# A limit of three on the loads under way in an agent-attention and soft-MoE kernel

## The chip, the cores and the metric

The kernel runs on one core of a Trainium2 chip. The core has engines that run side by side, each with its own instruction stream: TensorE for matrix products (PE in the profile; PEld is its loading of weights), VectorE (DVE), ScalarE (ACT), GpSimd (POOL) and SyncE (SP). Here SP computes nothing: it issues all DMAs, which move data between the device's memory and the on-chip memory on 16 DMA engines. The metric is the device time of one execution in microseconds (us); a lower one is better.

## The reference

Four batches (B = 4) of 11,456 rows with 128 channels pass through an agent attention with 49 agents, and all 45,824 rows of its result through a soft mixture of eight experts. Everything is in float32. Cut to what matters:

```python
def _attn_ref(q, k, v, agents):
    def sm(a, b):                       # softmax of scaled scores over the last axis
        s = scale * (a @ b.transpose(0, 2, 1))
        e = np.exp(s - s.max(-1, keepdims=True))
        return e / (e.sum(-1, keepdims=True) + 1e-09)
    a2k = sm(agents, k)
    agent_v = a2k @ v
    q2a = sm(q, agents)
    return q2a @ agent_v

def _moe_ref(x, phi, w1, w2):
    logits = x @ phi                    # N x 32 slots
    d = softmax of logits over the N rows
    slot_input = (d.T @ x).reshape(8, 4, 128)
    for e in range(8):
        slot_out[e] = np.maximum(slot_input[e] @ w1[e], 0.0) @ w2[e]
    c = softmax of logits over the 32 slots
    return c @ slot_out
```

## The kernel before, in words

A batch is cut into 90 cells of 128 rows. The k and v of a batch are read in five groups of up to 20 cells (`KGROUPS`), q in six groups of up to 16 (`GROUPS`). A group of k or of q is loaded transposed, 128 channels by cells x 128 rows, 64 KB a cell; a group of v has 129 columns a row, 64.5 KB a cell. There are 20 groups each of k and v, and 24 of q.

For each k group TensorE computes scores against the agents (`ks`, line 252), VectorE a running maximum, ScalarE the exponentials, and TensorE multiplies these with v (`kE`, line 351). For each q group TensorE computes scores (`qs`, line 466), the softmax over the agents follows on VectorE, ScalarE and GpSimd, then transposes (line 522) and the logits of the mixture (line 535). Rounds of two q groups or one gather the slots' inputs. When the last batch is through, the experts run (`mh`, line 805, with w1; `mo`, line 834, with w2), and a last loop forms the output and stores it in pieces of up to 1 MB (lines 994 to 1008).

The order of all steps is written out by hand in `ORDER`. Each token there is a step of one engine, and each engine takes its own steps in that order. `kx`, `kv` and `qx` are the loads of a k, v and q group, `cx` a load of constants, `w1` and `w2` those of the experts' weights. All go through SP, in order.

A load of a group is issued as DMAs of at most seven cells: 7, 7 and 6 cells for k and v (448, 448 and 384 KB, for v 451.5, 451.5 and 387), 7, 7 and 2 for q (448, 448 and 128 KB); a group of ten cells is 7 and 3. The function `load` (line 238) does it for k and q, `kv_` (line 285) for v:

```python
        for c0 in range(0, n, 7):
            c1 = min(c0 + 7, n)
            nc.sync.dma_start(out=xt[:, P * c0:P * c1],
                              in_=src[b, :, P * (ca + c0):P * (ca + c1)])
```

The buffers are few: two for k groups, three for v and three for q (`BUFS`: kt, vt, qt). A load into a buffer waits on SP until the last reader of what was there before is through; that reader is TensorE. Each DMA tells of its landing on one of eight semaphores, taken in turn, and before SP issues a DMA it waits for the one that used the semaphore before. The weights of the experts come at the end of the load stage: w1 and w2 each in four DMAs of 1 MB, two experts apiece, three of those of w2 into q buffers.

Of the kernel before, what the change touches and what calls it, by code (L numbers as in the profile page):

```python
# [17 lines left out]
P = 128  # L18
# [109 lines left out]
    "s": 4, "a": 3, "m": 1, "hs": 2, "ht": 3,  # L128
}
DEN_ACT = tuple(range(0, B * NG, 2))  # L130
FILL = (0, 4, 4, 3, 4, 3, 2)
CHUNKS = [4, 12] + [16] * 21 + [4, 4]
C0 = [sum(CHUNKS[:j]) for j in range(len(CHUNKS))]
# [40 lines left out]
def tile_agent_attn_soft_moe(ctx, tc, qT, kT, vL, agT, phi, w1, w2, cst, out):  # L174
    nc = tc.nc
# [48 lines left out]
    def op(fam, i, eng, cost, fn, deps=(), takes=(), gives=()):  # L224

        k = (fam,) + tuple(i)
        ops[k] = {"eng": eng, "cost": cost, "deps": list(dict.fromkeys(deps)), "takes": takes,
                  "gives": gives, "reads": {}}
        for tag, first in gives:
            ops[first]["reads"][tag] = ops[first]["reads"].get(tag, 0) + 1  # L230
        fns[k] = fn
        return k

    def tile_(tag, shape, name):
        return pools.get(tag, rp).tile(shape, F32, name=name,
                                       tag=f"{tag}{slots[tag, now[0]].pop(0)}", bufs=1)

    def load(tag, src, b, ca, cb, most):
        xt = tile_(tag, [P, most * P], f"{tag}_{b}_{ca}")
        n = cb - ca  # L240
        for c0 in range(0, n, 7):
            c1 = min(c0 + 7, n)
            nc.sync.dma_start(out=xt[:, P * c0:P * c1],
                              in_=src[b, :, P * (ca + c0):P * (ca + c1)])
        return xt

    def scores(b, xt, c0, c1, nm):

        sp = tile_("s", [P, c1 - c0, A], f"s{nm}")
        for c in range(c0, c1):  # L250
            for r in range(0, P, 64):
                t_.matmul(sp[r:r + 64, c - c0, :], xt[:, P * c + r:P * c + r + 64], ag[:, b, 0:A],  # L252
                          start=True, stop=True)
        return sp
# [12 lines left out]
    def k_ops(i):  # L267
        b, g = kgroups[i]
        ca, cb = KGROUPS[b][g]
        n, last = cb - ca, cb == NCELL  # L270
        cut = [(0, min(10, n))] + ([(10, n)] if n > 10 else [])
        k = {}
# [3 lines left out]
        def kx():  # L276
            if i:
                k["x"] = load("kt", kT, b, ca, cb, KC)
                return
            k["x"] = tile_("kt", [P, KC * P], "kt_0")  # L280
            for c0, c1 in ((ca, 4), (4, cb)):
                nc.sync.dma_start(out=k["x"][:, P * c0:P * c1], in_=kT[b, :, P * c0:P * c1])
            nc.sync.dma_start(out=cs[:, :P], in_=cst[:, :P])

        def kv_():
            k["v"] = tile_("vt", [P, KC, VC], f"vt_{i}")
            for c0 in range(0, n, 7):
                c1 = min(c0 + 7, n)
                nc.sync.dma_start(out=k["v"][:, c0:c1, :], in_=vL[b, :, ca + c0:ca + c1, :])

        def ks_(h):
            k["s", h] = scores(b, k["x"], *cut[h], f"k_{i}_{h}")
# [99 lines left out]
        def o(fam, sub, eng, cost, fn, **kw):  # L392
            return op(fam, (i,) + sub, eng, cost, fn, **kw)

        x = o("kx", (), "D", 156 * n, kx, takes=("kt",))
        v = o("kv", (), "D", 157 * n, kv_, takes=("vt",), deps=(x,))
        hs_ = range(len(cut))
        nh = [c1 - c0 for c0, c1 in cut]
# [43 lines left out]
    def q_ops(i):  # L442
# [17 lines left out]
        def qx():  # L460
            q["x"] = load("qt", qT, b, ca, cb, QC)[:, :P * n].rearrange("p (r x) -> p r x", r=4)
# [13 lines left out]
        def qm():  # L475
            q["mx"] = sm.tile([P, QC], F32, name=f"mx_{i}", tag="mx", bufs=6)
            v_.tensor_reduce(out=q["mx"][:, :n], in_=q["pt"][:, :n, 0:A], axis=AX.X, op=ALU.max,  # L477
                             negate=i in DEN_ACT)

# [103 lines left out]
        es, ps_, cc = [], [], []  # L583
        if i in DEN_ACT:
            for h in range(2):
# [101 lines left out]
    z, hps, hts, sos, w2s = {}, {}, {}, {}, {}  # L687
# [10 lines left out]
    def wl(name, shape, **kw):  # L698
        return z["wp"].tile(shape, F32, name=name, **kw)

    def z_w1(x):
        if x == 0:
            z["w1"] = wl("w1s", [P, E, F])
        nc.sync.dma_start(out=z["w1"][:, 2 * x:2 * x + 2, :], in_=w1[x])

    def z_w2(x):
        w2s[x] = (tile_("qt", [P, 2, F // P, C], f"w2s{x}") if x < 3 else
                  wl(f"w2s{x}", [P, 2, F // P, C]))
        nc.sync.dma_start(out=w2s[x], in_=w2[x])

    def z_ms():
        z["so"] = wl("so", [P, 2, C])
# [155 lines left out]
    def z_fl(n):  # L868
        fl = tile_("s", [P, 2, P], f"fl_{n}")
        for x in range(2):  # L870
            t_.transpose(fl[:, x], ident, ident)
# [9 lines left out]
    for x in range(4):  # L881
        wx.append(o("w1", "D", 2500, lambda x=x: z_w1(x), deps=ends + wx[-1:]))
    for x in range(4):
        wy.append(o("w2", "D", 2500, lambda x=x: z_w2(x), takes=("qt",) if x < 3 else (),
                    deps=ends + [("qx", NT - 1)] + wy[-1:]))
# [75 lines left out]
    f = None  # L961
    for n, d in enumerate([("qs", NT - 1, 1)] * FILL[0] + [("ql", NT - 1)] * FILL[1] +
                          [("r2", NR - 1)] * FILL[2] + [("r3", NR - 1)] * FILL[3] +
                          [w_] * FILL[4] + [gl] * FILL[5] + [b1] * FILL[6]):
        f = op("fl", (n,), "P", 214, lambda n=n: z_fl(n), deps=(d, f) if f else (d,),
# [103 lines left out]
```

## Time and profile before

| | |
|---|---|
| Median of three runs | 319.85 us (319.0 to 320.51) |
| The profiled execution | 321.17 us, its span 318.9 us |
| Busy PE, DVE, ACT, POOL in the span | 84%, 78%, 59%, 42% |
| Read from and written to the device's memory | 79.91 MB and 23.59 MB |
| Mean granted clock of TensorE | 0.931 |

The span is the time from the first to the last instruction of the profiled execution. It has three stages: to about 205 us loads and attention, to about 258 us the last rounds and the experts, and then the output. A row of the view by stretch gives, after the stretch's start and end, its length, the busy time of each engine with the number of its instructions, the granted clock, the share of the 16 DMA engines' time that was used (a little over 1 is full), and GB/s. A row of waits names who waited, for whom, the sum in us, how often and the longest. A row of DMA issues gives what is written from what, the number, the size of one and the median time from issue to landing. A row of the timeline gives the start, the length and the instruction. In the view of a line or a tile a row gives least, median and largest duration of an instruction in ns, and the first and the last start in us.

### The profile page before, as it was taken

The numbers are of one execution on the slowest core, as the hardware profiler recorded it, in microseconds if no ns is written. First come the engines' busy times: TensorE is split into PE (matmuls) and PEld (weight loads), VectorE is DVE, ScalarE is ACT, GpSimd is POOL, SyncE is SP. The second block draws the span as 40 slices with busy tenths as digits, with TensorE's granted clock in tenths as the row PEclk, the third lists the DMA queues.
The fourth block names the chain that finished last, engine by engine and source line by source line (L and its number), as shares of the span: only waits on it lengthen the run. The fifth ranks groups of instructions, "written<-read, shape, count | busy, mean of one in ns | idle before, by whom it ended". The sixth has DMA issues, their size and how long they took to land.

```text
span 318.9 us, 11055 instructions
## 1 busy us (share of the span) xinstructions
PE 266.3 (84%) x4522; PEld 169.4 (53%) x4522; DVE 248.1 (78%) x598; ACT 189.4 (59%) x623; POOL 132.5 (42%) x166
## 2 busy tenths in 40 slices
PE   3799999997698998988999998998898876766850
PEld 3638668665554776664666775565574632111210
DVE  1357767897769986988999988988999659989830
ACT  1125791492754985558589568698663255655550
POOL 1012223064505552566444490476897404434300
PEclk9999999999989999999999999999999997767555
DMA  7999999999979999867996899746930049999997
GB/s 250 400 402 390 398 396 402 401 397 400 394 250 376 399 393 368 301 260 295 377 377 264 252 360 384 244 175 237 419 141 3 2 164 422 415 415 420 420 419 286
DMA packets 31298, 104.20 MB, mean 327 GB/s; under 512 B 3601, under 2 KB 7825, under 8 KB 27537
## 3 DMA queue, kind: packets, MB, share of 16 engines
q1 hardware_dynamic: 31248, 103.52, 84.4%
q8 instruction: 35, 0.57, 0.7%
q14 instruction: 15, 0.11, 0.1%
HBM read 79.91 MB, written 23.59 MB: 325 GB/s over the span
## 4 chain that ended last, share of the span: by engine, by line
PE 45%; DVE 26%; DMA 10%; ACT 9%; issue 5%; POOL 2%; SPq 0%; DVEq 0%; POOLq 0%; ACTq 0%
PE sk L252 10%; PE ev L351 8%; PE sq L466 8%; DMA out<-ot 7%; PE tp L522 5%; ACT pt L494 4%; PE po L1002 3%; DVE pt L472 3%; PE lq L535 3%; DVE kmx L305 2%; ACT ot L1007 2%; DVE cd L852 2%; DVE ot L1006 2%; DMA w1s<-w 2%; DVE mx L477 2%
## 5 line engine op out<-in xcount | busy, mean ns | idle before, releaser
L494 ACT ACTIVATE pt<-pt,mx 128x49 f32<-128x49 f32 x192 | 61.6, 329 | 10.2 <-DVE mx L477 10.2
L513 POOL TENSOR_TENSOR pt<-pt,rt 128x392 f32<-128x392 f32 (+1 forms) x48 | 38.7, 809 | 46.1 <-DVE rt L508 25.2
L252 PE MATMUL sk<-ag,kt 128*64 128x49 f32 x1440 | 51.7, 230 | 6.6 <-DMA kt<-kT 4.3
L252 PEld LDWEIGHTS sk<-ag,kt 128*64 128x64 f32 x1440 | 48.8, 145 | 11.6 <-DVE ag L183 4.1
L466 PE MATMUL sq<-qt,ag 128*32 128x512 f32 (+1 forms) x384 | 49.6, 607 | 1.8 <-DVE et L339 1.1
L1002 PE MATMUL po<-ct,sob 32*128 32x512 f32 (+2 forms) x200 | 37.8, 838 | 15.6 <-DVE ct L865 11.3
L351 PE MATMUL ev<-vt,et 128*64 128x129 f32 x720 | 46.8, 277 | 1.7 <-issue 1.4
L1007 ACT COPY ot<-po 128x1536 f32<-128x1536 f32 (+2 forms) x25 | 32.8, 1311 | 23.3 <-DVE ot L1006 23.2
L351 PEld LDWEIGHTS ev<-vt,et 128*64 128x64 f32 x720 | 40.3, 138 | 9.6 <-issue 5.6
L472 DVE STREAM_TRANSPOSE pt<-sq 128x512 f32<-128x512 f32 (+1 forms) x48 | 31.9, 669 | 12.5 <-PE sq L466 12.0
L635 POOL TENSOR_TENSOR dt<-x_all,mbs 128x512 f32<-128x512 f32 (+1 forms) x24 | 29.2, 1227 | 28.8 <-DVE mbs L626 24.9
L859 POOL TENSOR_TENSOR x_all<-x_all,cd 128x512 f32<-128x512 f32 (+2 forms) x25 | 24.0, 961 | 38.0 <-DVE cd L854 37.3
L482 POOL TENSOR_TENSOR pt<-pt,mx 128x784 f32<-128x784 f32 (+1 forms) x12 | 16.2, 1353 | 55.4 <-DVE mx L477 53.1
L494 ACT ACTIVATION_READ_ACCUMULATOR pt<-pt,mx 128x1 f32 x192 | 37.0, 193 | 0.0
L529 ACT COPY pT<-tp 128x512 f32<-128x512 f32 (+1 forms) x48 | 25.7, 557 | 13.1 <-PE tp L522 11.0
L1002 PEld LDWEIGHTS po<-ct,sob 32*128 32x128 f32 x200 | 10.8, 247 | 42.5 <-ACT ot L1007 42.1
L522 PE MATMUL tp<-cs,pt 128*128 128x128 f32 x180 | 27.9, 286 | 5.9 <-issue 4.2
L305 DVE TENSOR_REDUCE kmx<-sk 128x49 f32<-128x490 f32 x32 | 20.7, 658 | 13.8 <-PE sk L252 13.6
L344 ACT ACTIVATE et<-et 128x490 f32<-128x490 f32 x36 | 21.6, 619 | 11.2 <-DVE et L339 11.1
L522 PEld LDWEIGHTS tp<-cs,pt 128*128 128x128 f32 x180 | 19.5, 142 | 15.1 <-issue 9.0
L339 DVE TENSOR_TENSOR et<-sk,kmb 128x490 f32<-128x490 f32 x36 | 22.5, 653 | 2.9 <-ACT kmb L329 2.8
L1006 DVE COPY ot<-po 128x512 f32<-128x512 f32 (+2 forms) x25 | 15.7, 629 | 11.4 <-DMA out<-ot 7.5
(111 smaller groups left out, 396.6 us busy)
## 6 DMA issues: line engine op xcount, KB each, us to landing
out<-ot SPq DMA_DIRECT2D x21, 1024.0 KB, 7.4
qt<-qT SPq DMA_DIRECT2D x44, 448.0 KB, 7.4
vt<-vL SPq DMA_DIRECT2D x36, 451.5 KB, 7.4
kt<-kT SPq DMA_DIRECT2D x35, 448.0 KB, 6.7
kt<-kT SPq DMA_DIRECT2D x17, 384.0 KB, 6.9
vt<-vL SPq DMA_DIRECT2D x16, 387.0 KB, 8.1
w2s<-w SPq DMA_DIRECT2D x4, 1024.0 KB, 6.9
w1s<-w SPq DMA_DIRECT2D x4, 1024.0 KB, 10.5
```

The costliest lines, as they stand in the source:

```text
L252: t_.matmul(sp[r:r + 64, c - c0, :], xt[:, P * c + r:P * c + r + 64], ag[:, b, 0:A], start=True, stop=True)
L305: v_.tensor_reduce(out=o_, in_=sp.rearrange("p c a -> p a c"), axis=AX.X, op=ALU.max)
L351: t_.matmul(k["ev"][o_:o_ + 64, :], k["e"][:, c, :], k["v"][:, c, :], start=c < 2, stop=c >= n - 2)
L466: t_.matmul(q["s", h][32 * r_:32 * r_ + 32, :nt], ag[:, b, 32 * h:32 * h + 32], q["x"][:, r_, :], start=True, stop=True)
L472: v_.transpose(out=q["pt"][:, :n, 32 * h:32 * h + 32], in_=q["s", h][:, :nt].rearrange("p (t a) -> p t a", a=32))
L494: s_.activation(out=x, in_=x, func=AF.Exp, bias=q["mx"][:, c:c + 1], accum_out=q["dn"][:, c:c + 1])
L513: nc.gpsimd.tensor_tensor(out=x, in0=x, op=ALU.mult, in1=q["rt"][:, c0:c1].unsqueeze(2).to_broadcast([P, c1 - c0, A]))
L522: t_.transpose(q["tp", h][:, (c - c0) // 2, :], q["pt"][:, c:c + 2, :].rearrange("p c a -> p (c a)"), ident)
L529: s_.copy(out=q["pT"][:, c0 // 2:c1 // 2, :], in_=q["tp", h][:, :(c1 - c0) // 2, :])
L635: nc.gpsimd.tensor_tensor(out=q["dt"][:, :n], in0=q["lt"][:, :n, :], op=ALU.subtract, in1=mbs[:, ri, :].unsqueeze(1).to_broadcast([P, n, S]))
L1002: t_.matmul(po[:, r, :32 * n], z["sob"][32 * r:32 * r + 32, :], z["ct", j][32 * r:32 * r + 32, :32 * n], start=True, stop=True)
L1007: s_.copy(out=ov[:, 1:4], in_=po[:, 1:4, :32 * n])
```

## The change

A list of the loads sent is kept. Every DMA of k, q, v, w1 and w2 goes through a new function `send`, which makes it wait until the one three places ahead of it in that list has landed. The DMAs of the agents and the constants and the stores do not go through it. The DMAs of w1 and w2 are cut in two, one for each expert, 512 KB each. Sizes and order of the other loads, buffers and `ORDER` stay.

```diff
+AHEAD = 3
@@
+    sent = []
+
+    def send(out, in_):
+
+        i = nc.sync.dma_start(out=out, in_=in_)
+        i = getattr(i, "ins", i)
+        if len(sent) >= AHEAD:
+            tc.add_manual_dep(i, sent[-AHEAD].name, mybir.DependencyInfo(
+                mybir.DependencyClass.Sync, mybir.DependencyReason.DATA), reason="load queue")
+        sent.append(i)
+
@@ def load
-            nc.sync.dma_start(out=xt[:, P * c0:P * c1],
-                              in_=src[b, :, P * (ca + c0):P * (ca + c1)])
+            send(xt[:, P * c0:P * c1], src[b, :, P * (ca + c0):P * (ca + c1)])
@@ def kx
-                nc.sync.dma_start(out=k["x"][:, P * c0:P * c1], in_=kT[b, :, P * c0:P * c1])
+                send(k["x"][:, P * c0:P * c1], kT[b, :, P * c0:P * c1])
@@ def kv_
-                nc.sync.dma_start(out=k["v"][:, c0:c1, :], in_=vL[b, :, ca + c0:ca + c1, :])
+                send(k["v"][:, c0:c1, :], vL[b, :, ca + c0:ca + c1, :])
@@ def z_w1
-        nc.sync.dma_start(out=z["w1"][:, 2 * x:2 * x + 2, :], in_=w1[x])
+        for e in range(2):
+            send(z["w1"][:, 2 * x + e], w1[x, :, e])
@@ def z_w2
-        nc.sync.dma_start(out=w2s[x], in_=w2[x])
+        for e in range(2):
+            send(w2s[x][:, e], w2[x, :, e])
```

## The prediction

> **What bounds the kernel now.** I first read the head of the page and its chain of waits, then the busy time by stretch.
>
> ```profile
> span 318.9 us, 11055 instructions
> ...
> PE 45%; DVE 26%; DMA 10%; ACT 9%; issue 5%; POOL 2%; SPq 0%; DVEq 0%; POOLq 0%; ACTq 0%
> ```
> ```profile
> core 0: us, PE busy (x) PEld busy (x) DVE busy (x) ACT busy (x) POOL busy (x), PEclk, DMA share, GB/s
> 0.00:30.00 30.00, 22.02 (x312) 15.54 (x312) 12.47 (x24) 6.66 (x21) 4.48 (x13) 1.00 0.96 360
> 30.00:88.00 58.00, 51.42 (x1060) 38.30 (x1062) 44.11 (x104) 36.25 (x148) 19.67 (x25) 0.99 1.03 397
> ...
> 88.00:130.00 42.00, 39.13 (x725) 27.57 (x727) 34.77 (x83) 28.14 (x116) 15.34 (x21) 0.97 0.96 358
> 130.00:157.00 27.00, 24.18 (x507) 15.93 (x507) 23.96 (x60) 17.73 (x61) 15.84 (x17) 1.00 0.82 301
> 157.00:205.00 48.00, 46.12 (x926) 31.21 (x920) 44.22 (x99) 35.86 (x149) 24.30 (x29) 1.00 0.87 313
> ```
>
> The chain is mostly PE, then DVE. By stretch, two things are nearly full at once: PE is busy 51.42 of 58 us and 46.12 of 48 us, and the DMA engines are full from 30 to 88 us (share 1.03, 397 GB/s) and nearly so to 130 us. After that the loads need only 301 to 313 GB/s. So PE sets the pace, with the loads just ahead of it: anything that lowers the rate of the loads below what these stretches ask will be seen.
>
> Next come the waits of SP, which issues all loads, and how many loads are under way at a time.
>
> ```profile
> SPq L243 <- PE sk L252: 21.1, 6, 6.5
> SPq L243 <- DMA kt<-kT: 17.5, 26, 1.4
> ```
> ```profile
> DMA packets 1334, 3.70 MB, mean 403 GB/s; under 512 B 148, under 2 KB 336, under 8 KB 1333
> ...
> vt<-vL SPq DMA_DIRECT2D x4, 451.5 KB, 8.0
> kt<-kT SPq DMA_DIRECT2D x2, 448.0 KB, 8.2
> ```
>
> SP already waits for landings, often and briefly (26 times, 1.4 us at most), and at other times for buffers that PE frees. The second fence is the DMA view of 53.3 to 62.5 us: a load lands 8.0 to 8.2 us after its issue while 403 GB/s flow. 8.1 us of that is 3.26 MB, some seven loads of 448 KB (0.459 MB). The kernel thus has seven or eight loads under way, and the change leaves three.
>
> **The change part by part.** *The wait.* It adds no work to a compute engine. What counts is how long a load takes when little is ahead of it, because with three under way each load is issued when the third before it has landed. The trace has seven such loads, issued after SP had stood waiting for a buffer and the queue had run low. They were issued at 174.77, 130.11, 199.88, 91.07, 144.07, 179.39 and 186.56 us; the first row places the first of them, and the others are in that order, issue to landing in the last column:
>
> ```profile
> 174.77 1.28 SPq L243 DMA_DIRECT2D kt<-kT  x3
> ```
> ```profile
> kt<-kT SPq DMA_DIRECT2D x1, 448.0 KB, 3.5
> ...
> vt<-vL SPq DMA_DIRECT2D x1, 451.5 KB, 3.3
> ...
> qt<-qT SPq DMA_DIRECT2D x1, 448.0 KB, 3.4
> ...
> qt<-qT SPq DMA_DIRECT2D x1, 448.0 KB, 3.3
> ...
> kt<-kT SPq DMA_DIRECT2D x1, 448.0 KB, 4.5
> ...
> vt<-vL SPq DMA_DIRECT2D x1, 451.5 KB, 4.2
> ...
> kt<-kT SPq DMA_DIRECT2D x1, 448.0 KB, 4.2
> ```
>
> Four take 3.3 to 3.5 us and three take 4.2 to 4.5. A 448 KB load takes 0.459 MB / 403 GB/s = 1.14 us of the engines' time, so a quiet load has about 2.2 us in which nothing of its own moves. Two others cover that only if they are large: 448 and 448 KB are 2.28 us, 448 and 384 KB 2.11, but 448 and 128 KB (the tail of a q group) only 1.46.
>
> The rate under the new limit follows. SP issues these loads:
>
> ```profile
> L243 SPq DMA_DIRECT2D qt<-qT x68: 327/328/1147, 5.9 to 200.7; - x68
> L243 SPq DMA_DIRECT2D kt<-kT x54: 327/328/597, 2.6 to 187.4; - x54
> L243 SPq EVENT_SEMAPHORE  x29: 17/17/28, 14.6 to 195.3; - x29
> ...
> L289 SPq DMA_DIRECT2D vt<-vL x56: 327/430/1519, 4.0 to 189.6; - x56
> ```
>
> With the first two of k that is 180 loads. By the kernel's sizes they carry 360 cells of 65,536 bytes for q, the same for k, and 66,048 bytes a cell for v: 70.96 MB, 0.394 MB a load, 1.183 MB for three. A group is read as 448, 448 and 384 or 128 KB, so the first load of a group nearly always waits for the first of the group before, both 448 KB, and three loads cannot land in less than one such time. At 3.4 us that is 1.183 / 3.4 = 348 GB/s; at 3.3 us 358; at 3.5 us 338; at the mean of all seven rows, 3.77 us, 314. I take 348, the middle of the quiet rows.
>
> Now the lag of the loads against before. To 88 us 30 x 360 + 58 x 397 = 33.8 MB were moved, which at 348 GB/s needs 97.2 us: 9.2 us late. From 88 to 130 us 15.0 MB need 43.2 us for 42: 10.4 us late. From 130 to 157 us 8.1 MB need 23.4 for 27, so up to 3.6 us can be won back, if SP's buffers are free. From there 313 GB/s is below 348 and the lag grows no more.
>
> What of it reaches PE is the lag less the time by which loads were early, and that is short in places. Issue, time to landing and first reader of the middle load of two q groups:
>
> ```profile
> 48.23 0.33 SPq L243 DMA_DIRECT2D qt<-qT  x1
> ...
> 148.53 0.44 SPq L243 DMA_DIRECT2D qt<-qT  x1
> ```
> ```profile
> qt<-qT SPq DMA_DIRECT2D x1, 448.0 KB, 7.4
> ...
> qt<-qT SPq DMA_DIRECT2D x1, 448.0 KB, 7.7
> ```
> ```profile
> 56.47 0.64 PE L466 MATMUL sq<-qt,ag 128*32 128x512 f32 x4
> ...
> 156.61 1.08 PE L466 MATMUL sq<-qt,ag 128*32 128x512 f32 x8
> ```
>
> 48.23 + 7.4 = 55.6 against 56.47: 0.9 us early. 148.53 + 7.7 = 156.2 against 156.61: 0.4 us. At 56 us the lag is (10.8 + 26 x 0.397 = 21.1 MB at 348 GB/s) 60.7 - 56 = 4.7 us, so PE would stand 3.8 us; by 157 us it has stood between 6.8 - 0.4 = 6.4 (all won back) and 10.4 - 0.4 = 10 us (nothing). I take 9, near the upper end: PE frees the buffers for which SP waits, and PE is itself late by then. Each third load also passes one more wake-up of SP (17 ns for the semaphore instruction): 60 x 0.02 = 1.2 us. Loads of the 4.2 us kind I charge at two more, about 0.9 us each over the quiet ones: 1.8. Sum: 9 + 1.2 + 1.8 = 12 us. The ends by the same sum: at 358 GB/s the lag at 157 us is 2.2 to 6.5 us, so 2 us at least; at 314 it is 19.7 at 88 us, 25.6 at 130 and about 24.5 at 157 and 205, so 25 us at most.
>
> Behind a waiting load SP holds only the later loads, the constants and, at the end, the stores; no other engine issues a DMA. The constants (two DMAs of lines 676 and 677, 336 and 16 KB by the kernel's sizes) don't pass through the limit and let it rise to five once, worth 0.36 MB / 403 GB/s = 0.9 us at most.
>
> *The halves of w1 and w2.* Eight DMAs of 1 MB become sixteen of 512 KB.
>
> ```profile
> L805 PE MATMUL hp<-w1s,si x32: 592/592/617, 244.7 to 250.1; 128*32 128x512 f32 x32
> L704 SPq DMA_DIRECT2D w1s<-w x4: 328/447/461, 217.3 to 219.9; - x4
> ...
> DMA to landing us min/median/max: 4.7/10.5/16.0
> ```
>
> The last w1 lands at 219.9 + 16.0 = 235.9 us; PE reads it from 244.7: 8.8 us to spare. Six MB go out from 217.3 us; at 348 instead of 403 GB/s these take 2.5 us more. I cost this at nothing: the softmax rounds of batch 3, in PE and DVE, hide it; without them it is 2.5 us. The order of all loads stays, and buffers are neither added nor taken.
>
> The profiled execution took 321.17 us (span 318.9 and 2.3 around it), 1.3 over the median of 319.85. Its sum is 333.2; against the median, which I predict, 319.85 + 12 = 332.
>
> **The rivals.** *Hidden anyway: 320 us.* Part of a load's fixed time may pass while the other two move, since the rows above are loads after a pause. For it: the first load of all, on an idle queue,
>
> ```profile
> ag<-agT SPq DMA_DIRECT2D x1, 128.0 KB, 2.2
> ```
>
> has 2.2 - 0.33 = 1.9 us that isn't its own bytes; 1.9 + 1.14 = 3.0 us gives 390 GB/s, 33.8 MB need 86.7 us and there is no lag. Against it: the four quiet 448 KB rows, none under 3.3. The Trainium skill, "DMA: Bandwidth & Descriptors", section "Anatomy of one DMA — SWDGE (gpsimd) path", fits 2.0 us plus the bytes at 436 GB/s for a DMA of the other issue path; that estimate is 3.05 us for 448 KB and lands on this rival, and the rows here are longer.
>
> *More than that: 345 us.* If most loads take what all seven rows take in the mean, the sum is the 25 us above. For it: three of seven; a late engine among the 16 can hold up a landing, and with three loads under way others can't run ahead. Against it: the four others, and that such delays are part of the stretches' rates before too.
>
> *Faster: 316 us.* PE stands where no releaser is shown, and instruction code comes through the same DMA engines:
>
> ```profile
> q8 instruction: 35, 0.57, 0.7%
> ```
> ```profile
> PE sk L252 <- DMA kt<-kT: 4.3, 2, 4.1
> PE tp L522 <- issue: 4.2, 2, 2.3
> ```
> ```profile
> 84.26 2.16 issue
> ```
>
> If that code queues behind eight loads, three would bring it sooner. "issue" is 5% of the chain; the two longest waits of this kind, ahead of the transposes (tp), are 4.2 us. These won and the lag hidden gives 319.85 - 4.2 = 316; it decides once what is won exceeds the lag, so only together with the first rival. Against it: the piece at 84 us is 2.16 us, not the 8 us of a full queue. The Trainium skill, same page, section "Queues, rings and completion order", says that a DMA engine takes turns between queues packet by packet; by that rule code never waits for the whole load queue and nothing is won. No run here shows it yet.
>
> *The change doesn't do what it says: 320 us.* The dependency might yield no wait. Against it: SP's waits for landings above are of the same kind, only further back.
>
> **How the numbers follow.** The forecast has 0.61 (own range 323 to 340), more than that 0.19, hidden 0.13, faster 0.04, no wait 0.03. A measurement tells about 0.5%, 1.6 us. Slower: 0.61 + 0.19 + 0.04 of the hidden case = 0.84; same: 0.08 + 0.03 = 0.11; faster: 0.04 + 0.01 = 0.05. The range goes from 320.5, which leaves out half of the hidden case and the faster one, to 346, the upper bound of the sum.
>
> **What would show it.** Issue to landing falls from 8 to 3.3 to 3.7 us; the rate from 30 to 88 us from 397 to near 350; SP's waits for landings grow to most of the load stage; PE waits for kt, vt or qt, now 4.3 us, by some 8 to 14 us more, with the first long ones at q groups between 45 and 60 us and again near 160. The stores at the end keep their length. It would be wrong if the rate stays near 397 (hidden), or if it stays low and PE doesn't wait, so that the loads had more time to spare than the two places show.

## The result, and the profile after

| | before | after |
|---|---|---|
| Median | 320.18 us (319.0 to 322.73) | 386.75 us (386.13 to 389.52) |
| Ratio, 95% interval | | 1.208 (1.199 to 1.218) |
| The profiled execution, its span | 321.17 us, 318.9 | 389.52 us, 387.6 |

The change costs 66.6 us, 5.5 times the 12 us of the forecast, and the time lies far above the range. Now and then an execution of a kernel is slower by a few per cent; medians here and below take in all executions, ratios and intervals only the others. The page of the kernel after, its span and its chain of waits, by engine and by line:

```profile
span 387.6 us, 11059 instructions
...
DMA 71%; PE 13%; DVE 8%; ACT 5%; issue 1%; SPq 1%; DVEq 0%
DMA qt<-qT 25%; DMA vt<-vL 22%; DMA kt<-kT 16%; DMA out<-ot 6%; DVE ot L1019 2%; PE sq L477 2%; DMA w1s<-w 2%; PE ev L362 2%; DVE cd L865 2%; ACT ot L1020 2%; PE hp L818 1%; ACT pt L505 1%; DVE ct L878 1%; PE tp L533 1%; PE so_p L847 1%
```

PE, which made up 45% of the chain before, has 13%; the loads of q, v and k have 63%. The loads have become the path that sets the end. The view by stretch of the kernel after, with the columns as before (length, busy time of the engines, granted clock, DMA share, GB/s):

```profile
30.00:88.00 58.00, 43.22 (x674) 28.49 (x674) 28.50 (x68) 26.97 (x119) 9.16 (x13) 0.94 0.82 270
88.00:130.00 42.00, 32.62 (x544) 22.43 (x544) 24.13 (x55) 16.21 (x58) 13.69 (x17) 0.84 0.78 247
...
0.00:273.00 273.00, 211.10 (x3504) 142.55 (x3504) 160.55 (x368) 125.91 (x494) 79.56 (x105) 0.90 0.82 264
```

From 30 to 88 us 270 GB/s flow where 397 did, and it stays so through the load stage: 264 GB/s in the mean, at a DMA share of 0.82. The DMA issues of the kernel after, with the median time to landing in the last column:

```profile
out<-ot SPq DMA_DIRECT2D x21, 1024.0 KB, 7.5
qt<-qT SPq DMA_DIRECT2D x44, 448.0 KB, 4.2
vt<-vL SPq DMA_DIRECT2D x36, 451.5 KB, 4.7
kt<-kT SPq DMA_DIRECT2D x35, 448.0 KB, 4.3
```

A load of 448 KB lands after 4.2 to 4.7 us. That is little over half of the 8.0 to 8.2 us in the view from 53.3 to 62.5 us before, but not the 3.4 us on which the sum was built. What this does is seen in the chain of waits from 55 to 75 us of the kernel after, in order of time (start, length, what):

```profile
52.04 4.12 DMA vt<-vL
56.16 0.02 issue
56.18 4.31 DMA qt<-qT
60.49 0.02 issue
60.51 4.28 DMA kt<-kT
...
69.55 0.02 issue
69.57 5.29 DMA qt<-qT
74.86 0.04 issue
74.90 0.62 PE sq L477
```

Each piece is one load, and between two of them there is nothing but SP's wake-up of 0.02 us. Every load here waits for the third before it, and PE waits for the last. The same in the sums of the waits, first SP's, then PE's:

```profile
SPq L239 <- DMA kt<-kT: 71.0, 54, 3.7
...
SPq L239 <- DMA vt<-vL: 66.0, 55, 3.5
SPq L239 <- DMA qt<-qT: 58.9, 51, 2.5
```
```profile
PE sq L477 <- DMA qt<-qT: 34.0, 15, 5.6
...
PEld sq L477 <- DMA qt<-qT: 18.5, 23, 2.3
PE sk L263 <- DMA kt<-kT: 15.8, 11, 4.3
```

SP stands 196 us for landings. PE's matrix products wait 34.0 + 15.8 = 49.8 us for q and k, where the largest such row before was 4.3 us. The time at which the last load of q goes out shows that hardly anything was lost later:

```profile
L239 SPq DMA_DIRECT2D qt<-qT x68: 327/328/433, 11.5 to 269.1; - x68
```

It goes out at 269.1 us instead of 200.7, 68.4 us later. The span has grown by 68.7 us. All but 0.3 us of the loss was made in the load stage.

### The profile page after: what moved, and what is told of

It is laid out like the page before. It is cut to its first block, busy times and chain, and to the rows that moved or that the text cites. A ratio compares the mean times of both kernels' runs of the same rounds, so it can differ in the third digit from the quotient of the medians.

```text
span 387.6 us, 11059 instructions
## 1 busy us (share of the span) xinstructions
PE 293.0 (76%) x4522; PEld 183.9 (47%) x4522; DVE 249.3 (64%) x598; ACT 190.3 (49%) x623; POOL 132.4 (34%) x166
## 4 chain that ended last, share of the span: by engine, by line
DMA 71%; PE 13%; DVE 8%; ACT 5%; issue 1%; SPq 1%; DVEq 0%
DMA qt<-qT 25%; DMA vt<-vL 22%; DMA kt<-kT 16%; DMA out<-ot 6%; DVE ot L1019 2%; PE sq L477 2%; DMA w1s<-w 2%; PE ev L362 2%; DVE cd L865 2%; ACT ot L1020 2%; PE hp L818 1%; ACT pt L505 1%; DVE ct L878 1%; PE tp L533 1%; PE so_p L847 1%
## 5 line engine op out<-in xcount | busy, mean ns | idle before, releaser
L477 PE MATMUL sq<-qt,ag 128*32 128x512 f32 (+1 forms) x384 | 70.2, 647 | 34.8 <-DMA qt<-qT 34.0
L263 PE MATMUL sk<-ag,kt 128*64 128x49 f32 x1440 | 56.7, 240 | 16.9 <-DMA kt<-kT 15.8
L263 PEld LDWEIGHTS sk<-ag,kt 128*64 128x64 f32 x1440 | 53.0, 155 | 23.5 <-issue 10.7
L362 PE MATMUL ev<-vt,et 128*64 128x129 f32 x720 | 48.9, 287 | 1.4 <-DMA vt<-vL 1.3
L1015 PE MATMUL po<-ct,sob 32*128 32x512 f32 (+2 forms) x200 | 33.6, 751 | 19.5 <-DVE ct L878 12.7
L362 PEld LDWEIGHTS ev<-vt,et 128*64 128x64 f32 x720 | 42.8, 144 | 9.6 <-issue 4.4
L477 PEld LDWEIGHTS sq<-qt,ag 128*32 128x32 f32 x384 | 15.2, 116 | 60.8 <-issue 29.7
L1015 PEld LDWEIGHTS po<-ct,sob 32*128 32x128 f32 x200 | 10.0, 227 | 43.0 <-ACT ot L1020 42.7
```

Of the source, the lines that this page charges most:

```text
L362: t_.matmul(k["ev"][o_:o_ + 64, :], k["e"][:, c, :], k["v"][:, c, :], start=c < 2, stop=c >= n - 2)
L477: t_.matmul(q["s", h][32 * r_:32 * r_ + 32, :nt], ag[:, b, 32 * h:32 * h + 32], q["x"][:, r_, :], start=True, stop=True)
L1015: t_.matmul(po[:, r, :32 * n], z["sob"][32 * r:32 * r + 32, :], z["ct", j][32 * r:32 * r + 32, :32 * n], start=True, stop=True)
```

## The experiments

The letters in the expectations are theories. A: with few loads under way the time of a load grows with its companions, so bytes under way set the rate, and starting a load costs the DMA engines time of their own. B: a load simply takes 4.5 us beside the compute engines, whatever the limit. C: the work of the compute engines, or instruction code, slows the loads. D: the number of loads under way counts, not their size. E: larger DMAs gain by themselves. F: a short load queue lets TensorE's instruction code come sooner.

### Limits of one, two and four

```diff
-AHEAD = 3
+AHEAD = 1        # and 2, and 4
```

> A limit of one load under way in place of three; nothing else differs from the changed kernel. Theory A (companions): a load alone takes the 3.4 us of the quiet rows, and it is the other two under way that stretch it to the 4.5 us of the changed kernel, because a landing waits for the slowest of 16 DMA engines and every later load waits for the landing. Then the 448 KB loads here take 3.3 to 3.5 us, the 128 KB ones about 2.3, all 180 about 570 us, and the time is about 570 + 114 = 685 us. Theory B (loads are just slower): a 448 KB load takes 4.5 us whenever the kernel computes beside it, and the quiet rows were the short end of that. Then 448 KB loads take 4.3 to 4.6 us here too and the time is about 880 us.

> A limit of two. Theory A (companions): a load takes between 3.4 and 4.5 us, about 3.9, two land in that time, 90 x 3.9 = 351 us of loads and about 465 us in all. Theory B (loads are just slower): 4.5 us, 405 us of loads, about 520 us.

> A limit of four. Theory A (companions): each further load under way stretches the others again, to about 5.1 us; four loads of 0.394 MB in 5.1 us are 309 GB/s, 230 us of loads and about 345 us. Theory B (loads are just slower): 4.5 us as with three, 350 GB/s, 203 us of loads as before the change, 318 to 324 us.

Measured: 724.51 us with a limit of one and 460.41 with two (one execution each), 345.55 with four, 1.075 times before (1.067 to 1.084); the rows for four come from an execution of 352.29 us. The stretch rows and the q loads of each, limit one first:

```profile
50.00:550.00 500.00, 252.64 (x3183) 150.78 (x3184) 145.20 (x337) 118.21 (x470) 73.61 (x91) 0.67 0.43 123
```
```profile
qt<-qT SPq DMA_DIRECT2D x44, 448.0 KB, 3.4
```
```profile
30.00:330.00 300.00, 206.82 (x3264) 131.94 (x3266) 148.31 (x343) 118.33 (x471) 74.45 (x92) 0.85 0.71 210
```
```profile
qt<-qT SPq DMA_DIRECT2D x44, 448.0 KB, 4.0
```
```profile
30.00:220.00 190.00, 165.43 (x2988) 114.00 (x2986) 135.57 (x323) 109.05 (x425) 71.59 (x88) 0.95 0.90 307
```
```profile
qt<-qT SPq DMA_DIRECT2D x44, 448.0 KB, 5.0
```

A load of q that is truly alone takes 3.4 us in the median, with one companion 4.0, with two 4.2, with three 5.0. So the prediction's quiet rows were right as rows: they are the time of a lone load. They are not the time of a load with two others ahead of it. B falls: the time depends on the limit. A was right on two and four, and 40 us short on one. That run's last q load goes out at 584.6 us, later than the 570 us expected for all loads, and 138 us lie behind it against 118.5 after the change; the loads of w1 and w2, one at a time, lie there.

The traces show which part of a load comes late. They hold sixteen marks of completion for each load, and SP's next issue follows 0.02 us after the last. With a limit of one the first mark of a load of seven cells comes 2.84 us after its issue, the eighth after 3.09, the fifteenth after 3.30 and the last after 3.40 (medians of 114 loads); with three they come after 2.86, 3.26, 4.04 and 4.33 (115 loads). Half of a load is hardly later than alone; its last parts are, and the next load waits for these. Why they are late no run here took apart.

### Loads alone

This kernel leaves all computation out: it issues loads of 448 KB of k, 24 for each limit, and fills the output with zeros. Its total time means nothing.

```diff
+STAGES = (1, 2, 3, 4, 5, 8)
+EACH = 24
+        for ahead in STAGES:
+            for _ in range(EACH):
+                b, c = (j // 12) % B, CELLS * (j % 12)
+                send(bufs[j % 16], kT[b, :, P * c:P * (c + CELLS)], ahead)
+                j += 1
```

> A kernel that leaves out all of the reference's computation: SP alone loads 24 pieces of 448 KB each under a limit of 1, 2, 3, 4, 5 and 8, one limit after the other, into 16 buffers that nobody reads in between; zeros are stored at the end. Theory A (companions): issue to landing 3.3 to 3.5 us under a limit of 1, 4.3 to 4.6 under 3, so that the engines alone make the delay, without any compute. Theory B (loads are just slower beside compute): 3.4 us under every limit up to 3, about 400 GB/s under 3. The same 3.4 under 1 and 3 with 4.5 in the changed kernel would make the computing engines or their code loads the cause (theory C).

The view by stretch, one row within the stage of each limit (length, busy DVE and POOL, clock, DMA share, GB/s):

```profile
10.00:80.00 70.00, 0.00 (x0) 0.00 (x0) 1.00 0.46 132
85.00:125.00 40.00, 0.00 (x0) 0.00 (x0) 1.00 0.78 224
132.00:162.00 30.00, 0.00 (x0) 0.00 (x0) 1.00 0.92 310
168.00:195.00 27.00, 0.00 (x0) 0.00 (x0) 1.00 1.00 365
197.00:220.00 23.00, 0.00 (x0) 0.00 (x0) 1.00 1.03 408
226.00:248.00 22.00, 12.02 (x12) 0.00 (x0) 1.00 1.03 406
```

From issue to landing, with a limit of one and of three:

```profile
ld<-kT SPq DMA_DIRECT2D x22, 448.0 KB, 3.4
...
ld<-kT SPq DMA_DIRECT2D x21, 448.0 KB, 4.3
```

With three under way 310 GB/s flow though nothing else runs, and a load of k takes the same 4.3 us as in the kernel after. The prediction's rule was that three loads of the kernel, 1.183 MB, take the time of one of 448 KB. By it the 3 x 0.459 / 0.310 = 4.44 us found here make 266 GB/s, and the kernel had 264. C falls as the cause: the time is there without any computation. That the compute engines add a few tenths of a us, to the loads of v (4.7 us) for instance, no run rules out. Five loads of 448 KB, 2.3 MB, fill the engines.

The share tells a part of why the companions don't cover the start of a load. One load takes 0.459 MB / 132 GB/s = 3.48 us at a limit of one, and at a share of 0.46 that is 1.60 us of the engines' packet time; at a limit of five it is 1.12 us x 1.03 = 1.16. So a lone load pays some 0.44 us more packet time. With two under way all of it is still paid (2.05 x 0.78 = 1.60 us), with three 0.20 of it (1.48 x 0.92 = 1.36), with four 0.10 (1.26 x 1.00 = 1.26). With three a load comes every 1.48 us, 0.36 later than with five: 0.20 of that is this packet time, and the rest is time in which the engines stand (the share is 0.92 against 1.03). The Trainium skill, "DMA: Bandwidth & Descriptors", section "Rules for kernel authors", says that the fixed setup cost overlaps with computation when a DMA is issued early. It doesn't say whether other loads cover it too; in these rows they do so fully only from five on. Whether an engine could have served another load in the added packet time no run here shows.

### Sizes under a limit, loads alone

The same kernel without computation, 20 loads for each pair of limit and cells (64 KB a cell).

```diff
-STAGES = (1, 2, 3, 4, 5, 8)
+STAGES = ((3, 2), (3, 4), (3, 7), (3, 14), (3, 20), (5, 4), (6, 4), (8, 4))
```

> Loads alone, with all of the reference's computation left out: 20 pieces each under (limit, cells of 64 KB) = (3, 2), (3, 4), (3, 7), (3, 14), (3, 20), (5, 4), (6, 4), (8, 4). Theory A: under three the rate rises with the size, about 110 GB/s at two cells, 200 at four, 300 at seven as before, and 400 at 14 and 20; five of four cells give 280 to 320, near three of seven, as the kernel with small pieces did; eight of four cells 400. The engine time of a load is that of its bytes plus about 0.4 us where the engines ran dry. Theory D: five of four cells reach 400.

The view by stretch, one row within each stage in that order:

```profile
3.00:14.00 11.00, 0.00 (x0) 0.00 (x0) 1.00 0.60 177
20.00:34.00 14.00, 0.00 (x0) 0.00 (x0) 1.00 0.82 253
42.00:62.00 20.00, 0.00 (x0) 0.00 (x0) 1.00 0.90 305
72.00:106.00 34.00, 0.00 (x0) 0.00 (x0) 1.00 1.01 413
120.00:165.00 45.00, 0.00 (x0) 0.00 (x0) 1.00 1.01 424
172.00:186.00 14.00, 0.00 (x0) 0.00 (x0) 1.00 0.96 347
191.00:201.00 10.00, 0.00 (x0) 0.00 (x0) 1.00 1.03 360
206.00:214.00 8.00, 0.00 (x0) 0.00 (x0) 1.00 1.05 395
```

Three at a time give 177, 253, 305, 413 and 424 GB/s as a load grows from 128 to 1280 KB; 256 KB loads reach 395 with eight. So number and size both raise the rate. Bytes under way order most of it: 1.3 to 1.4 MB (three of 448, five of 256 KB) give 305 and 347, 2.1 MB (eight of 256) 395, 2.8 MB (three of 896) 413. They are not the whole of it: three of 128 KB, 0.39 MB, give 177, where one of 448 KB, 0.46 MB, gave 132. At small sizes the numbers expected were too low, for five of 256 KB too. Theory D, 400 GB/s there, fails with 347.

By its mean size alone, 385 KB, the kernel after would lie between 253 and 305, near 290 GB/s; it had 264. Its small loads are held up by the large ones: those of 128 KB land after 3.7 us there, and three of 128 KB alone after 2.2. That fits the rule of the 448 KB load above, but no run has the kernel's mixture of sizes without its computation.

The Trainium skill, "DMA: Bandwidth & Descriptors", section "Measured (HBM→SBUF, 128 partitions, SWDGE, issued from GpSimd)", asks for at least 1 MiB a DMA. With a short queue the rows agree (from 305 to 413 GB/s), with eight under way 256 KB are nearly enough.

### Smaller pieces, and a limit of five

```diff
-AHEAD = 3
+AHEAD = 5
-        for c0 in range(0, n, 7):
-            c1 = min(c0 + 7, n)
+        for c0 in range(0, n, 4):
+            c1 = min(c0 + 4, n)
```

> Pieces of four cells (256 KB) in place of seven under a limit of five: 1.3 MB under way at most, about what three pieces of the changed kernel hold (1.2 MB), but five DMAs. Theory A (bytes under way, and a start-up for each load): the rate stays near that of the limit of three, 260 to 290 GB/s, and the time is 360 to 390 us. Theory D (the number under way decides, as each landing is a fixed time behind its issue): the rate is that of a limit of five, 340 GB/s or more, and the time is 320 to 330 us.

Measured: 363.59 us, in one execution. Its row by stretch:

```profile
30.00:88.00 58.00, 49.37 (x807) 31.98 (x803) 32.57 (x77) 29.05 (x124) 11.89 (x16) 0.94 0.92 300
```

Five of 256 KB hold 1.3 MB under way, like three of 448, and give 300 GB/s instead of 270; five of 448 KB filled the engines. D falls. A holds in the kernel too, though the rate lies a little over the 260 to 290 that it gave.

### The halves of w1 and w2 alone

```diff
-AHEAD = 3
+AHEAD = 1000     # no wait is ever added; the cuts of w1 and w2 stay
```

> The halves of w1 and w2 alone: no load waits for another one by the limit, everything else is as in the changed kernel. All theories: the prediction costed this part at nothing, with 8.8 us to spare before the experts read w1, so 320 us, within 0.5% of before. Over 322 us would mean that a part of the loss belongs to the halves.

Measured: 321.06 us, 1.003 times before (0.9996 to 1.007). The halves cost nothing that can be told.

### Whole groups under a limit of three, and what came of the gain

```diff
-        for c0 in range(0, n, 7):
-            c1 = min(c0 + 7, n)
+        for c0 in range(0, n, 20):
+            c1 = min(c0 + 20, n)
```

The same is done for v. A group of k, v or q is now one DMA, 1024 to 1290 KB.

> The limit of three as changed, but each group of k, q and v is one DMA (up to 20 cells, 1280 KB) and not three. Theory A, now in the form 'the start of a load costs 0.4 us of the engines' own time, and three loads of 394 KB are too few bytes to hide the rest': three loads are up to 3.9 MB, the engines never run dry, the rate is 390 to 400 GB/s, and the time is 320 to 325 us (a little over before, since a reader waits for a whole group). If the number of loads under way were the limit whatever their size, three loads a 4.5 us would still be up to 790 GB/s, so this run only asks whether bytes cure it; a time over 340 us would mean that the waiting on SP itself is what costs.

Measured: 315.77 us, 0.987 times before (0.979 to 0.994), from four executions. The limit alone, on loads of this size, takes nothing:

```profile
30.00:88.00 58.00, 53.70 (x1096) 39.08 (x1098) 45.85 (x108) 37.28 (x151) 19.71 (x25) 1.00 1.00 404
```

With three groups, some 3.7 MB, under way the engines are full again. The same wait that costs 66 us on 448 KB loads costs nothing here, which shows that the wait itself was never the price. These are a third as many loads, but a limit of six on all 180 loads of the kernel after, below, costs nothing either. The gain of 1.3% was not expected. Of the six runs that follow five asked where it came from, and the one with a limit of two asked whether bytes alone count.

```diff
-AHEAD = 3
+AHEAD = 1000     # whole groups without a limit; then 2, 4, and 3 again
```

> One DMA for each group and no limit; otherwise the kernel of the whole groups under a limit of three, which took 315.8 us. It tells whether the gain over before is that of the large DMAs or that of the limit. Theory E (large DMAs): fewer starts and fewer semaphores, 315 to 317 us here too. Theory F (the limit: with less queued, what else uses the DMA engines, the instruction code of TensorE above all, comes sooner): 319 to 321 us here.

> One DMA for each group under a limit of two. Theory A (bytes under way): two of up to 1280 KB are 2.2 MB in the mean, more than the 2.0 MB of five small loads, which filled the engines with loads alone; the time stays within 1% of the limit of three, 314 to 320 us. If the number under way decided (theory D), two would be as slow as the limit of two with small loads, over 400 us.

> One DMA per group of k, v and q, and each load waits for the landing of the load four ahead of it (limit 4 where the run with whole groups at limit 3 took 0.987 of the time before and the one without a limit 1.000). Up to 5 MB under way, so the load stage stays full: 30 to 88 us at 395 to 405 GB/s. Theory A (only the bytes under way count): 318 to 321 us, as without a limit. Theory F (a short load queue lets the instruction code of TensorE come sooner; idle time of TensorE put down to no releaser was 42 us with the limit of three and 57 us without one): between the two, 316 to 319 us, with that idle time between 42 and 57 us.

> The run with whole groups at limit 3 once more, on another chip and with more rounds, since its gain (0.987 of the time before) rests on four executions and the same kernel with limit 4 lost it (1.004). Theory F (a short load queue lets the code of TensorE come sooner): 314 to 318 us, and idle time of TensorE put down to no releaser near 42 us again (52 before, 57 without a limit, 48 at limit 4). Rival (scatter: the order in which work falls into place differs by chance between executions, and with it some us): 318 to 321 us, idle time of that kind between 45 and 57 us.

Then seven cells with a limit of six, and ten cells (640 KB) with a limit of five:

```diff
-AHEAD = 3
+AHEAD = 6        # pieces of seven cells; in the second run 5, and
-        for c0 in range(0, n, 7):
-            c1 = min(c0 + 7, n)
+        for c0 in range(0, n, 10):
+            c1 = min(c0 + 10, n)
```

> The changed kernel with a limit of six. Theory A: six loads are 2.4 MB, the engines don't run dry, and the time is that of before, 319 to 323 us. Theory D: the same. A gain over before, below 318 us, would speak for theory F, that a shorter queue helps other users of the DMA engines.

> Pieces of up to ten cells (640 KB; 10 and 6 for q) with limit 5: some 2.9 MB under way, between six loads of seven cells (2.4 MB, 0.995 of the time before) and three whole groups (3.7 MB, 0.987). Theory F: 315 to 318 us. Rival (scatter, or only the bytes under way count): 318 to 321 us. Under both 385 to 405 GB/s from 30 to 88 us.

| loads, limit | median us | ratio to before, 95% interval |
|---|---|---|
| whole groups, 2 | 334.18 | 1.030 (1.022 to 1.039) |
| whole groups, 3 | 315.77 | 0.987 (0.979 to 0.994) |
| whole groups, 3, again | 319.99 | 0.997 (0.992 to 1.001) |
| whole groups, 4 | 322.06 | 1.004 (1.001 to 1.008) |
| whole groups, none | 320.1 | 1.000 (0.997 to 1.003) |
| ten cells, 5 | 323.11 | 1.012 (1.006 to 1.018) |
| seven cells, 6 | 319.19 | 0.995 (0.992 to 0.998) |

E falls: without a limit large loads gain nothing. F does not hold up either. The first run looked like it: PE's waits with no releaser shown ("issue", PE and PEld together) sum to 41.9 us there, against 51.5 before and 56.6 without a limit. But limit four has 48.4, fewer than before, and is slower. The same kernel on another chip has 42.3 again, as F expected, and its profiled execution took 320.90 us; it kept 0.3% of the 1.3%, with 1 in its interval. So that idle time can fall by 9 us and the time stay. What made the first four executions short stays open: two of them, 314.2 and 314.6 us, lie below all twelve of the second run (315.8 to 321.7). Scatter or the chip may be the cause; neither is shown. Ten cells with a limit of five missed both expectations, and why isn't known. Apart from the first run of whole groups, which did not repeat, no version beat the kernel before by more than half a per cent.

Whole groups with a limit of two were expected to cost nothing, and cost 3%. Their row:

```profile
30.00:88.00 58.00, 48.79 (x929) 36.21 (x927) 38.65 (x91) 30.75 (x127) 15.39 (x20) 0.94 0.94 345
```

Up to 2.6 MB under way, 2.2 in the mean, give only 345 GB/s, though five loads of 448 KB, 2.3 MB, gave 408 alone. In the kernel six loads, 2.4 MB in the mean, moved 387 GB/s from 30 to 88 us. SP's waits with whole groups and a limit of two are for landings in this stretch, hardly for buffers:

```profile
SPq L239 <- DMA kt<-kT: 19.9, 5, 5.0
SPq L239 <- DMA vt<-vL: 17.3, 6, 3.3
SPq L239 <- DMA qt<-qT: 14.1, 5, 4.1
SPq L239 <- PE t L270: 0.3, 1, 0.3
```

So the loads themselves were slow. With two, one landing leaves half of the bytes in the queue, with five four fifths: a reading that fits both rates, but that no run took apart.

## Why the prediction was wrong

**Right.** That the loads ran just ahead of PE from 30 to 130 us, so that a lower rate would be seen; that the wait is real and that the rate is the bytes of three loads by the time of one; that the halves cost nothing that can be told; that the stores keep their length (7.4 us before, 7.5 after). The side was right: slower.

**The step that failed** is the one that sized a load's time: "At 3.4 us that is 1.183 / 3.4 = 348 GB/s". It measured 1.183 / 0.264 = 4.48 us, and the median rows are 4.2 to 4.7. The 3.4 us came from rows of loads after a pause, with little or nothing left ahead of them; the run with a limit of one has shown that this is the time of a load alone. The sentence ahead of it, that two companions cover the "2.2 us in which nothing of its own moves", took the fixed part as a delay that leaves the engines free and the companions as no hindrance to the load itself. Loads alone showed both wrong: the time of a load, its issue included, goes from 3.48 to 3 x 0.459 / 310 GB/s = 4.44 us when two others are under way. Of the delay, 0.2 us a load stands as packet time, and the marks of completion show that it is the last parts of a load that are late.

**The rest of the sum was sound.** Its own working with 4.48 us, 264 GB/s: 33.8 MB take 128.0 us, 40.0 late at 88; 15.0 MB take 56.8 for 42, 54.8 late; 8.1 MB take 30.7 for 27, 58.5 late; the 48 us from 157 at 313 GB/s are 15.0 MB and take 56.8, so 67.3 late at 205. Measured: 68.4. At 348 GB/s the lag ended at 130 us, because the need fell to 313; at 264 it never ends, and that is why an error of a third in one term became a factor of five and a half in the result. Since 264 is the mean rate of just this stage, its sum has to come out; with the 266 GB/s from loads alone the same four stretches give some 65 us. The time by which loads were early, 0.4 to 0.9 us, no longer mattered.

**The range.** The rival "more than that" named the right mechanism, a late part that holds up a landing, and took 3.77 us, the mean of the seven rows. The three long rows are of this kind: of the load issued at 144.07 us fifteen marks were there after 3.31 us and the last after 4.50. They were charged as exceptions, 1.8 us in all, and under the limit late parts are the rule. Companions don't tell the long rows from the quick ones. The load at 174.77 us, 3.5 us long, had nothing ahead of it and others right behind it, and so had the one of 4.5 us. The 345 us was the upper end of the range, and no row was taken as the bound for a load with two loads ahead of it. The bound was there. The third load after the pause at 174.77 us went out behind two that were still under way:

```profile
kt<-kT SPq DMA_DIRECT2D x1, 384.0 KB, 4.8
```

If three loads take that long, the rate is 1.183 / 4.8 = 246 GB/s. A straight line gives the same: with seven or eight under way a load took 8.1 us, alone 3.4, so each companion adds (8.1 - 3.4) / 6.5 = 0.7 us, and two make 4.8. Either would have been nearer than every number that was used.

**The other rivals.** "Hidden anyway" fails. The fit of the Trainium skill, "DMA: Bandwidth & Descriptors", section "Anatomy of one DMA — SWDGE (gpsimd) path", which is for the other issue path, made 3.05 us of a 448 KB load; from SP a load alone takes 3.4, so the fit doesn't carry over. "Faster" through code was not seen. "No wait" fails by SP's 196 us of waits for landings.

**What would show it.** Issue to landing was to fall to 3.3 to 3.7 us and fell to 4.2 to 4.7; the rate to near 350, and was 270; PE's waits for loads were to grow by 8 to 14 us, and grew by some 45; the first longer one for q, 3.5 us, came between 45 and 62 us as forecast. SP's waits grew as said.

The cut of w1 kept its cover, if less of it. The loads of w1 and their reader after:

```profile
L818 PE MATMUL hp<-w1s,si x32: 592/838/1062, 313.2 to 319.1; 128*32 128x512 f32 x32
L239 SPq DMA_DIRECT2D w1s<-w x8: 327/328/432, 285.8 to 303.1; - x8
...
DMA to landing us min/median/max: 4.1/5.1/5.8
```

The last lands by 303.1 + 5.8 = 308.9 us, and PE reads from 313.2: 4.3 us to spare instead of 8.8.

## What to carry to other kernels

A limit on the loads under way is a limit on the rate: size it by bytes and number under way (here five loads of 448 KB or three of 900 KB filled the engines), and take the time of a load from rows with as many loads ahead of it as it will have, not from the first row after a pause. Where only the lone and the crowded load are in the trace, a line between the two may serve for the first estimate; for three companions it gives 5.5 us here, where 5.0 were measured. Where the new rate lies near what a later stretch needs, work the sum on both sides of that point: below it the lag grows to the end of the stage.

## What was not expected of the hardware

- With few loads under way a load costs the DMA engines more packet time, not only more waiting: 1.60 us for 448 KB alone or with one other, 1.36 with two others, against 1.16 with four.
- With two others under way it is the last parts of a load that come late: of its sixteen marks of completion the eighth moves from 3.09 to 3.26 us, the last from 3.40 to 4.33.
- The granted clock of TensorE fell with its waiting: from 0.99 between 30 and 88 us before to 0.94 with a limit of three, and to 0.67 in the load stage with a limit of one. The Trainium skill, "TensorE: Matmul & The Clock Gate", section "Part 1: The HAM clock gate (the "warmup" mystery)", says that the clock is halved after an idle window of some 3.4 us; waits of PE for q were up to 5.6 us here. The traces agree: behind these means the granted clock is 1.0 or 0.5, in stretches of 3.4 us or multiples of it. Since the loads set the end, none of the 68.4 us was traced to the clock.
- Two large loads under way move less (345 GB/s with up to 2.6 MB) than more small ones of about as many bytes (408 with 2.3 MB in five, loads alone; 387 with 2.4 in six, in the kernel).
